# Rounding up the small tiles ahead of the matmul operands, so that every tile begins on a multiple of 64 bytes of a partition

## The chip, the cores and the metric

The kernel runs on one core of one Trainium2 chip. The metric is the device time of one execution in microseconds; lower is better. TensorE's clock has two levels, 1.2 and 2.4 GHz; the profile gives the granted share of full speed. Tiles lie in on-chip memory, 128 partitions side by side; a tile has the same start in every partition, and "where a tile begins" means its byte offset within a partition.

## The reference

Three modules in a row on 8 sequences of 576 tokens of width 512, all in fp32. The second module's two weights are multiplied by 8 in the inputs.

```python
def _attn_ref(q, k, v, g_norm):                 # 8 heads of 64
    kv = np.einsum('bhsd,bhse->bhde', k, v)
    out = np.einsum('bhsd,bhde->bhse', q, kv)
    rms = np.sqrt(np.mean(out * out, axis=-1, keepdims=True) + 1e-06)
    return (out / rms * g_norm).astype(np.float32)

def _moe_ref(x, w_ch1, w_ch2):                  # 512 -> 2048 -> 512
    X = np.fft.fft(np.fft.fft(x, axis=1), axis=2)
    u = x + np.real(X).astype(np.float32)
    un = (u - mean(u)) / np.sqrt(var(u) + 1e-06)
    return (u + np.maximum(un @ w_ch1, 0.0) @ w_ch2).astype(np.float32)

def _moe2_ref(x, U, V, w_ch1, w_ch2):           # rank 32 over the sequence
    h = x.transpose(0, 2, 1) @ U @ V
    u = x + h.transpose(0, 2, 1)
    return (u + np.maximum(u @ w_ch1, 0.0) @ w_ch2).astype(np.float32)
```

## The kernel before, in words

The 8 x 576 = 4608 tokens form 9 blocks of 512 (`BT`). The hidden width 2048 is cut into 16 slabs of 128 (`NF`). To keep fp32 accuracy with fast matmuls, each fp32 operand is split into a high part and a low remainder, both of type fp32r, and a product is three matmuls: low by high, high by low, high by high. Nearly all large matmuls therefore have 128x128 weights and stream 128x512 elements of 4 bytes.

**First transform (blocks 0 to 8).** For each of the 9 x 16 slabs `emit_l1` (L204) runs 12 matmuls: weights w1h and w1l, streamed xh and xl; ScalarE and VectorE make gh and gl from the result; `emit_l2` (L219) then runs 12: weights are slices of gl and gh, streamed w2h and w2l. Besides, ScalarE, VectorE and GpSimd split the weights of slabs to come, and beside each block of 16 slabs the attention and the Fourier transforms of the next sequence are placed (`batch_tasks`): t_kv, t_o, folds, two small DFT matmul stages against tables (t_s1, t_s2), and transposes of the normalized tokens (t_tr).

**Second transform.** Its first block, block 9 of the same loop, is plain: `emit_l1` streams xhb and xlb (tiles of pool `pb`) against w1h and w1l, and `emit_l2` now takes w2l, w2h as weights and streams gh, gl (L234 to L236). The other eight blocks go in four groups of two (`group`, L873), each with a fast 2x2 scheme of seven products instead of eight. A group's first phase (L953) has 56 units of 6 matmuls in the order `P1`: weights v, which are loaded from DRAM into five buffers of `pb`, streamed xv. There are seven variants p of xv (`XTAG`): 0, 1, 4 and 5 lie in pool `pa`, in the tiles xh, xl, res, un; 2, 3 and 6 in `pb`, in x0, x1, x2. p = 1 writes z, 3 and 6 write zz, the others y. ScalarE and VectorE (`post1`) empty the results into the 32 tiles of `wpool`. The phase ends with two units, (2, 7) and (6, 7), that follow each other. The second phase (L1033) has 56 units of 6 in the order `P2`: weights v, streamed high and low parts that `make` (L930) writes five units ahead (`LEAD`) into the buffers of w1h/w1l, w2h/w2l and gh/gl in turn, two buffers of each. In groups 1 to 3 the first phase also holds projecting matmuls of t_pt (L649: weights u1, streamed x2s), and units 2 to 9 of the second phase stand between transposes of t_u2 (L671, L674), all for the next group.

The order on every engine is that of the program's text (`tc.manual_schedule`): each engine goes through its list and waits where an operand isn't there. DMAs are issued by SyncE.

**Where tiles lie.** Pools are laid out one after the other in the order in which they are opened: com, wsp, gpool, pa, wpool, cvp and then at (attention), whose place pb takes later. In a pool tiles follow each other in the order of first use. Starts are rounded up to 32 bytes. com begins with ident (512 bytes), xe0 (96), nhalf (32), muT (144) and kvbd; because of the small ones, kvbd and all that follows in wsp, gpool and pa begins 32 bytes past a multiple of 64. pa ends with three small tiles (ln6, ln2, ln1: 96, 32, 16 bytes), after which wpool, cvp and pb begin on multiples of 64.

Of the kernel before, what the change touches and what calls it, by code (L numbers as in the profile page):

```python
# [10 lines left out]
F32 = mybir.dt.float32  # L11
F32R = mybir.dt.float32r
# [7 lines left out]
B, H, S, D = 8, 8, 576, 64  # L20
NH = S // 2 + 1
DM, DFF, RANK = 512, 2048, 32
NT = B * S
C = 128
RL = NH - 2 * C
NQ = 4 * C + 98
NS = 290
ND = 258
# [15 lines left out]
def kernel(ctx: ExitStack, tc: tile.TileContext, qT, kvm, gn, w1a, w2a, w1b, w2b,  # L44
# [4 lines left out]
    com = ctx.enter_context(tc.tile_pool(name="com", bufs=1))  # L49
# [7 lines left out]
    pa = ctx.enter_context(tc.tile_pool(name="pa", bufs=1))  # L57
    wpool = ctx.enter_context(tc.tile_pool(name="wpool", bufs=NF))
    cvp = ctx.enter_context(tc.tile_pool(name="cvp", bufs=1))

    early = [True]

    def side_bank(nm):
        if early:
            k = len(early) % 6
            early.append(True)
            if k < 4:
                return ps_acc.tile([128, 512], F32, tag=f"acc{k}", name=nm)
        return ps_s.tile([128, 512], F32, tag="side", name=nm)
# [6 lines left out]
    ub_d = [dram.tile([DM, BT], F32, tag=f"ub_d{j}", name=f"ub_d{j}") for j in range(1, NB)]  # L76

    ident = com.tile([128, 128], F32, name="ident")
    xe0 = com.tile([C, 3, B], F32, name="xe0")
    nhalf = com.tile([128, 8], F32, name="nhalf")  # L80
    muT = com.tile([128, NT // 128], F32, name="muT")


    def raw_load(src, n, where=None):
# [157 lines left out]
    at = att_ctx.enter_context(tc.tile_pool(name="at", bufs=1))  # L242
# [5 lines left out]
    def load_tables(step, t={}):  # L248

        for k, src in enumerate(tabs):  # L250
            if step == 0:
                t[k] = dram.tile(list(src.shape), F32, tag=f"tab_d{k}", name=f"tab_d{k}")
                nc.sync.dma_start(out=t[k], in_=src)
                continue
            s = at.tile(list(src.shape), F32R, name=f"tab{k}")
            nc.sync.dma_start(out=f32(s), in_=t[k])
            o = 0
            for nm, p, n in TABS[k]:
                tb[nm] = s[0:p, o:o + n]
                o += n  # L260
                if nm[1] in "sd":
                    tb[nm] = tb[nm].rearrange("p (k n) -> p k n", k=2)
# [24 lines left out]
    def t_o(b, k):  # L287
        s = st[b]
        g, c, m = OT[k]
        if k == 0:  # L290
            s["x"] = at.tile([C, 2, 3, DM], F32, tag="xpn", name=f"x{b}")
            s["sq"] = at.tile([C, 5, DM], F32, tag="slot_b", name=f"sq{b}")
            s["ss"] = at.tile([C, 5, H], F32, tag="ss", name=f"ss{b}", bufs=2)
        ps = side_bank(f"o{b}_{k}")
        for j in range(4):
            nc.tensor.matmul(out=ps[:m, 128 * j:128 * j + 128], lhsT=s["q"][:, j, C * k:C * k + m],  # L296
                             rhs=kvbd[:, j, :], start=True, stop=True)
        nc.scalar.activation(out=s["sq"][:m, k, :], in_=ps[:m, :], func=AF.Square)
        heads = lambda v: v.rearrange("p (h d) -> p h d", d=D)
        nc.vector.tensor_tensor(out=heads(s["x"][:m, g, c]), in0=heads(ps[:m, :]),  # L300
                                in1=gnb[:m].unsqueeze(1).to_broadcast([m, H, D]), op=ALU.mult)
        ss = s["ss"][:m, k]
        nc.vector.reduce_sum(out=ss, in_=s["sq"][:m, k].rearrange("p (h d) -> p h d", d=D), axis=AX.X)
        nc.vector.tensor_scalar(out=ss, in0=ss, scalar1=1.0 / D, scalar2=EPS, op0=ALU.mult, op1=ALU.add)
        nc.gpsimd.tensor_tensor(out=ss, in0=ss, in1=nhalf[:m, :], op=ALU.pow)
# [90 lines left out]
    def t_s2(b, c):  # L396
        s = st[b]
        m = min(C, NS - C * c)
        y = s["y"]
        pss = []  # L400
        for p in range(2):
            th, tl = (tb["cdh"], tb["cdl"]) if p == 0 else (tb["sdh"], tb["sdl"])
            ps = side_bank(f"s2_{b}_{c}_{p}")
            pss.append(ps)
            for ec in range(2):
                a, l = (y[:, p, k, ec, C * c:C * c + m] for k in range(2))
                nc.tensor.matmul(out=ps[:m, :ND], lhsT=l, rhs=th[:, ec, :], start=(ec == 0), stop=False)
                nc.tensor.matmul(out=ps[:m, :ND], lhsT=a, rhs=tl[:, ec, :], start=False, stop=False)
                nc.tensor.matmul(out=ps[:m, :ND], lhsT=a, rhs=th[:, ec, :], start=False, stop=(ec == 1))
        de = at.tile([C, 3, ND], F32, tag="de", name=f"de{b}_{c}", bufs=2)  # L410
        nc.scalar.activation(out=de[:m, 0], in_=pss[1][:m, :ND], func=AF.Copy)
        nc.vector.tensor_tensor(out=de[:m, 1], in0=pss[0][:m, :ND], in1=de[:m, 0], op=ALU.subtract)
        nc.vector.tensor_tensor(out=de[:m, 2], in0=pss[0][:m, :ND], in1=de[:m, 0], op=ALU.add)
        for g in range(2):
            x = s["x"][:m, g, c]
            eng = nc.vector if b == 0 and g == 0 else nc.gpsimd
            eng.tensor_tensor(out=x[:, 0:257], in0=x[:, 0:257], in1=de[:m, 1 + g, 0:257], op=ALU.add)
            eng.tensor_tensor(out=x[:, 257:512], in0=x[:, 257:512], in1=de[:m, 2 - g, 255:0:-1], op=ALU.add)
        if b:
            t_u_out(b, c)  # L420

    def t_u_out(b, c):
        s = st[b]
        n0, n1 = C * c, min(C * c + C, 289)
        nc.sync.dma_start(out=u_d[b][n0:n1, :], in_=s["x"][0:n1 - n0, 0, c])
        n0, n1 = C * c, min(C * c + C, 288)
        nc.sync.dma_start(out=u_d[b][288 + n0:288 + n1, :], in_=s["x"][n0 - C * c:n1 - C * c, 1, c])

    def load_q(b):
        q = at.tile([128, 4, NQ], F32, tag="slot_c", name=f"q{b}")  # L430
        nc.sync.dma_start(out=q, in_=qT[b])
        st.setdefault(b, {})["q"] = q

# [7 lines left out]
    def batch_tasks(b):  # L441

        t = [[] for _ in range(14)]
        d = SH if b == 1 else 0
        for c in range(3):
            ks = range(2 * c, min(2 * c + 2, 5))
            t[c + d] += [lambda k=k: t_o(b, k) for k in ks]
            t[c + d + 1] += [lambda k=k: t_norm(b, k) for k in ks]
            t[c + d + 3] += [lambda c=c, p=p: t_fold_s(b, c, p) for p in range(2)]
            t[c + d + 3] += [lambda c=c: t_fold_e(b, c, 0), lambda c=c: t_fold_h(b, c, 0)]  # L450
            t[c + d + 4] += [lambda c=c: t_fold_e(b, c, 1), lambda c=c: t_fold_h(b, c, 1)]
            t[c + d + 4] += [lambda p=p, c=c: t_fold_l(b, c, p) for p in range(2)]
            t[c + 9].append(lambda c=c: t_s2(b, c))
        for p in range(2):
            t[8 if d else 7 + p] += [lambda p=p, e=e: t_s1(b, p, e) for e in range(2)]
        if b + 1 < B:
            t[6 + d].append(lambda: load_kv(b + 1))
            t[11].insert(0, lambda: t_kv(b + 1, 0))
            t[12].insert(0, lambda: t_kv(b + 1, 1))
            t[12].append(lambda: load_q(b + 1))  # L460
        return t
# [18 lines left out]
    lns = {}  # L480
# [23 lines left out]

    def t_ln_stats(j, ts):
        if j not in lns:
            lns[j] = [pa.tile([128, 4, w], F32, tag=f"ln{w}", name=f"ln{j}_{w}") for w in (6, 2, 1)]
        st6, mv, rs = lns[j]
        for t in ts:
            nc.vector.bn_stats(out=st6[:, t, :], in_=un[j][t])  # L510
            nc.vector.bn_aggr(out=mv[:, t, :], in_=st6[:, t, :])
# [544 lines left out]
    with tc.manual_schedule():  # L1056
# [4 lines left out]
        nc.scalar.activation(out=e288, in_=f32(e288), func=AF.Copy)  # L1061
        load_kv(0)
        load_q(0)
        nc.sync.dma_start(out=gnb, in_=gn)
        load_tables(0)
        for s in range(4):
            w_load(s)
        load_tables(1)
        done = 0

# [8 lines left out]
        for k in range(5):  # L1079
            t_o(0, k)  # L1080
# [17 lines left out]
        conv_b(*conv_a(raws.pop(0), w_new(0), pws.pop(0)))  # L1098
        w_mags(1)
        t_s2(0, 2)  # L1100
        t_ln_first(2)
        t_s2(0, 0)
        t_ln_first(0)
        t_s2(0, 1)
# [5 lines left out]
        done = 2  # L1110
        load_kv(1)
        load_q(1)
        t_ln_stats(0, (0, 2))
        t_ln_stats(0, (1, 3))
        t_ln(0)
        for t in range(4):
# [67 lines left out]
        for n in range(NP):  # L1184
            i, j = n % NF, n // NF
# [136 lines left out]
```

## Time and profile before

| | |
|---|---|
| runs shown | 1823.01 us median of 3 (1821.85 to 1826.5) |
| profiled execution | 1822.28 us, of which the span of the trace is 1820.5 |
| mean granted clock | 0.982 |
| busy: PE, PEld, DVE, ACT, POOL | 95%, 79%, 65%, 46%, 26% of the span |
| DMA | 318 MB, 175 GB/s on average |
| stages, us from the span's start | first transform to 1052, block 9 to 1158, groups 1 to 4 from 1158, 1325, 1493 and 1659 |

PE is TensorE's matmul, PEld its weight load, which overlaps matmuls. A matmul's duration in the trace covers its way through the array, and the next one starts long before it ends; what counts in a stream is the distance between two starts. In the timeline and in the chain a row is one instruction or several of one kind merged (x6), with the first one's start and the time of all.

### The profile page before, as it was taken

To read this page: it belongs to the slowest core of one execution; us is meant where nothing else is said; L and a number is where in the kernel's file an instruction comes from. 1 tells how busy PE (TensorE), PEld (TensorE's weight loads), DVE (VectorE), ACT (ScalarE), POOL (GpSimd) and SP (SyncE) were. 2 spreads that over 40 slices of the span, in tenths; PEclk is the share of its full clock that TensorE was granted. 3 is DMA by queue.
4 is the path that set the end of the run, shared out by engine and by line. 5 is a ranking of instruction groups with operands and counts; after the bars stand their busy time and mean duration, and the time that the engine had idled before them with its cause. 6 is when DMAs were issued, how large, how long until landed. Compare 5 with 4: busy or idle time off the path is not lost.

```text
span 1820.5 us, 22972 instructions
## 1 busy us (share of the span) xinstructions
PE 1737.2 (95%) x8136; PEld 1432.6 (79%) x8136; DVE 1191.6 (65%) x1918; ACT 830.0 (46%) x1584; POOL 478.7 (26%) x384
## 2 busy tenths in 40 slices
PE   5678999999999999999999989999999999999999
PEld 5557778888787887878888868888887888888877
DVE  5787875857758586574476676637934873595285
ACT  4565343444534344343445466355535534453243
POOL 2556544454445544344222212100000000000000
PEclk7889999999999999999999999999999999999999
DMA  6735423143241513302258875566785776677675
GB/s 251 248 95 200 141 104 138 59 163 122 102 141 61 209 58 130 122 12 73 65 202 282 298 278 205 179 200 221 223 274 171 246 247 201 208 232 237 189 220 185
DMA packets 123731, 318.18 MB, mean 175 GB/s; under 512 B 18056, under 2 KB 20632, under 8 KB 120608
## 3 DMA queue, kind: packets, MB, share of 16 engines
q1 hardware_dynamic: 123616, 316.72, 52.2%
q8 instruction: 64, 1.05, 0.2%
q14 instruction: 51, 0.42, 0.1%
HBM read 241.13 MB, written 77.17 MB: 175 GB/s over the span
## 4 chain that ended last, share of the span: by engine, by line
PE 76%; DVE 12%; ACT 4%; DMA 3%; issue 2%; POOL 2%; SPq 1%; ACTq 0%; POOLq 0%; DVEq 0%
PE y L953 10%; PE yy L1033 10%; PE h L210 5%; PE h L212 5%; PE h L211 5%; PE acc L230 5%; PE acc L232 5%; PE z L1033 5%; PE acc L231 5%; PE zz L953 5%; PE z L953 2%; PE w L1033 2%; DVE f L335 2%; PE o L296 2%; DVE eh L364 2%
## 5 line engine op out<-in xcount | busy, mean ns | idle before, releaser
L188 POOL TENSOR_TENSOR w1l<-w,w1h 128x512 fp32r<-128x512 f32 x148 | 196.0, 1325 | 445.6 <-ACT w1h L187 422.2
L230 PE MATMUL acc<-w2h,gl 128*128 128x512 f32 x576 | 232.0, 403 | 28.8 <-DVE gl L216 28.7
L231 PE MATMUL acc<-w2l,gh 128*128 128x512 f32 x576 | 230.0, 399 | 8.4 <-POOL w2l L196 8.4
L210 PE MATMUL h<-xl,w1h 128*128 128x512 f32 x576 | 229.1, 398 | 1.4 <-DVE xl L533 1.4
L232 PE MATMUL acc<-w2h,gh 128*128 128x512 f32 x576 | 229.4, 398 | 0.0
L212 PE MATMUL h<-xh,w1l 128*128 128x512 f32 x576 | 225.5, 391 | 0.0
L211 PE MATMUL h<-xh,w1h 128*128 128x512 f32 x576 | 225.3, 391 | 0.0
L953 PE MATMUL y<-xv,v 128*128 128x512 f32 x768 | 192.2, 396 | 2.7 <-ACT g L890 2.7
L215 ACT ACTIVATE gh<-h 128x512 fp32r<-128x512 f32 x160 | 94.5, 591 | 179.6 <-PE h L212 177.3
L953 PEld LDWEIGHTS y<-xv,v 128*128 128x128 f32 x768 | 143.9, 188 | 38.9 <-ACT g L890 4.5
L216 DVE SCALAR_TENSOR_TENSOR gl<-h,gh 128x512 fp32r<-128x512 f32 x160 | 109.6, 686 | 98.8 <-ACT gh L215 98.5
L890 ACT ACTIVATE g<-y 128x512 f32<-128x512 f32 x128 | 76.6, 599 | 212.7 <-PE y L953 212.7
L196 DVE TENSOR_TENSOR w2l<-w,w2h 128x512 fp32r<-128x512 f32 x144 | 126.3, 877 | 48.9 <-ACT w2h L195 48.4
L230 PEld LDWEIGHTS acc<-w2h,gl 128*128 128x128 f32 x576 | 110.7, 192 | 60.1 <-DVE gl L216 37.1
L231 PEld LDWEIGHTS acc<-w2l,gh 128*128 128x128 f32 x576 | 110.6, 192 | 33.2 <-POOL w2l L196 11.0
L232 PEld LDWEIGHTS acc<-w2h,gh 128*128 128x128 f32 x576 | 111.0, 193 | 23.3
L212 PEld LDWEIGHTS h<-xh,w1l 128*128 128x128 f32 x576 | 108.5, 188 | 24.1
L210 PEld LDWEIGHTS h<-xl,w1h 128*128 128x128 f32 x576 | 108.8, 189 | 22.7 <-DVE xl L533 1.8
L211 PEld LDWEIGHTS h<-xh,w1h 128*128 128x128 f32 x576 | 108.7, 189 | 20.9
L195 ACT ACTIVATE w2h<-w 128x512 fp32r<-128x512 f32 x160 | 99.8, 624 | 38.9 <-PE acc L232 35.3
L187 ACT ACTIVATE w1h<-w 128x512 fp32r<-128x512 f32 x160 | 99.7, 623 | 14.7 <-DVE w L118 14.7
L884 DVE TENSOR_TENSOR g<-zz,g 128x512 f32<-128x512 f32 x64 | 44.2, 691 | 94.1 <-ACT g L890 80.7
(213 smaller groups left out, 3600.2 us busy)
## 6 DMA issues: line engine op xcount, KB each, us to landing
v<-wv_d SPq DMA_DIRECT2D x224, 512.0 KB, 4.0
wv_d<-vo SPq DMA_DIRECT2D x112, 256.0 KB, 2.8
kv<-in_kvm SPq DMA_DIRECT2D x14, 1280.0 KB, 9.4
q<-in_qT SPq DMA_DIRECT2D x8, 1220.0 KB, 9.3
x_d<-x2o SPq DMA_DIRECT2D x36, 256.0 KB, 2.1
x2f<-x_d SPq DMA_DIRECT2D x36, 256.0 KB, 5.2
outT<-o SPq DMA_DIRECT2D x36, 256.0 KB, 3.0
u_d<-x SPq DMA_DIRECT2D x32, 256.0 KB, 2.7
```

The source lines that it names most:

```text
L188: (nc.vector if n in on_dve else nc.gpsimd).tensor_tensor(out=al, in0=a, in1=f32(ah), op=ALU.subtract)
L195: nc.scalar.activation(out=ch, in_=c, func=AF.Copy)
L196: (nc.gpsimd if n in CLP else nc.vector).tensor_tensor(out=cl, in0=c, in1=f32(ch), op=ALU.subtract)
L210: nc.tensor.matmul(out=h, lhsT=ah[:, kc, :], rhs=xl[:, kc, :], start=(kc == 0), stop=False)
L211: nc.tensor.matmul(out=h, lhsT=ah[:, kc, :], rhs=xh[:, kc, :], start=False, stop=False)
L212: nc.tensor.matmul(out=h, lhsT=al[:, kc, :], rhs=xh[:, kc, :], start=False, stop=(kc == 3))
L216: nc.vector.scalar_tensor_tensor(out=gl, in0=h, scalar=0.0, in1=f32(gh), op0=ALU.max, op1=ALU.subtract)
L230: nc.tensor.matmul(out=a, lhsT=gl[:, tt], rhs=ch, start=s, stop=False)
L231: nc.tensor.matmul(out=a, lhsT=gh[:, tt], rhs=cl, start=False, stop=False)
L232: nc.tensor.matmul(out=a, lhsT=gh[:, tt], rhs=ch, start=False, stop=e)
L953: nc.tensor.matmul(out=dst, lhsT=w[:, c], rhs=r[:, k], start=p in (0, 1, 3) and k + n == 0, stop=k == 1 and n == 2, skip_group_check=True)
L1033: nc.tensor.matmul(out=dst[mp], lhsT=w[:, c], rhs=r, start=p in (0, 1, 6, 3) and i + n == 0, stop=i == 7 and n == 2, skip_group_check=True)
```

## The change: what it does

A helper, whole, allocates a tile with its row rounded up to 16 elements (64 bytes) and returns a view of the wanted part. It is used for xe0, nhalf, muT (pool com), ln6, ln2, ln1 (pa), and in at for the three tables, ss, de and q. No other tile changes its size. The views have the shape of the tiles before, so every instruction keeps its shape; and the engines' instructions stand in the same order, with the same waits. What changes is the start of tiles, here by its remainder modulo 64 bytes:

| tiles | before | after |
|---|---|---|
| kvbd; wsp: w1h, w1l, w2h, w2l; gpool: gh, gl | 32 | 0 |
| pa: xh, xl, un, res, x2o | 32 | 0 |
| wpool: w0, w1; cvp: raw, cv1 | 0 | 0 |
| at: gnb, e288, slot_a (kv, f), slot_c (q, y) | 0 | 0 |
| at: tables, x, slot_b (sq, eh), ez, one of the two de | 32 | 0 |
| pb: o, u1, x0, x1, x2, vs, v, x2f | 0 | 0 |

Among the tiles of wsp, gpool and pa the distances stay as they are. Rows within a tile keep their own offsets: 2048 or 512 bytes for the large operands, multiples of 8 bytes for some slices of the tables, of y and of q.

```diff
+    def whole(pool, shape, dt, name, tag=None, bufs=1):
+
+        n = int(np.prod(shape[1:]))
+        t = pool.tile([shape[0], -(-n // 16) * 16], dt, tag=tag or name, name=name, bufs=bufs)[:, 0:n]
+        if len(shape) == 2:
+            return t
+        names = "abcd"[:len(shape) - 1]
+        return t.rearrange(f"p ({' '.join(names)}) -> p {' '.join(names)}", **dict(zip(names, shape[1:])))
...
-    xe0 = com.tile([C, 3, B], F32, name="xe0")
-    nhalf = com.tile([128, 8], F32, name="nhalf")
-    muT = com.tile([128, NT // 128], F32, name="muT")
+    xe0 = whole(com, [C, 3, B], F32, "xe0")
+    nhalf = whole(com, [128, 8], F32, "nhalf")
+    muT = whole(com, [128, NT // 128], F32, "muT")
...
-            s = at.tile(list(src.shape), F32R, name=f"tab{k}")
+            s = whole(at, list(src.shape), F32R, f"tab{k}")
...
-            s["ss"] = at.tile([C, 5, H], F32, tag="ss", name=f"ss{b}", bufs=2)
+            s["ss"] = whole(at, [C, 5, H], F32, f"ss{b}", "ss", 2)
...
-        de = at.tile([C, 3, ND], F32, tag="de", name=f"de{b}_{c}", bufs=2)
+        de = whole(at, [C, 3, ND], F32, f"de{b}_{c}", "de", 2)
...
-        q = at.tile([128, 4, NQ], F32, tag="slot_c", name=f"q{b}")
+        q = whole(at, [128, 4, NQ], F32, f"q{b}", "slot_c")
...
-            lns[j] = [pa.tile([128, 4, w], F32, tag=f"ln{w}", name=f"ln{j}_{w}") for w in (6, 2, 1)]
+            lns[j] = [whole(pa, [128, 4, w], F32, f"ln{j}_{w}", f"ln{w}") for w in (6, 2, 1)]
```

## Rows read from the trace of the kernel before

**Rows 1.** The page: busy time of TensorE, granted clock in 40 slices.

```profile
PE 1737.2 (95%) x8136; PEld 1432.6 (79%) x8136; DVE 1191.6 (65%) x1918; ACT 830.0 (46%) x1584; POOL 478.7 (26%) x384
...
PEclk7889999999999999999999999999999999999999
```

**Rows 2.** The page: the chain that ended last, shares of the span by engine.

```profile
PE 76%; DVE 12%; ACT 4%; DMA 3%; issue 2%; POOL 2%; SPq 1%; ACTq 0%; POOLq 0%; DVEq 0%
```

**Rows 3.** TensorE's waits, whole run: total us, times, longest.

```profile
PE acc L230 <- DVE gl L216: 28.7, 20, 2.7
...
PE y L953 <- ACT g L890: 2.7, 4, 0.7
```

**Rows 4.** TensorE in order of time, first transform: start, us, instruction.

```profile
900.15 0.39 PE L232 MATMUL acc<-w2h,gh 128*128 128x512 f32 x1
...
903.55 0.39 PE L212 MATMUL h<-xh,w1l 128*128 128x512 f32 x1
```

**Rows 5.** The chain within group 4's second phase: start, us, instructions.

```profile
1749.48 11.20 PE z L1033 x48
```

**Rows 6.** Stretches: us, PE busy (instructions touched), clock, DMA share, GB/s.

```profile
880.00:948.00 68.00, 67.01 (x296) 1.00 0.50 163
1270.00:1321.00 51.00, 51.00 (x221) 1.00 0.72 224
```

**Rows 7.** TensorE in order of time, block 9, first and second layer.

```profile
1111.85 0.40 PE L211 MATMUL h<-xhb,w1h 128*128 128x512 f32 x1
...
1114.43 0.39 PE L234 MATMUL acc<-gh,w2l 128*128 128x512 f32 x1
...
1115.59 0.39 PE L236 MATMUL acc<-gh,w2h 128*128 128x512 f32 x1
...
1116.94 0.40 PE L236 MATMUL acc<-gh,w2h 128*128 128x512 f32 x1
```

**Rows 8.** The chain within group 1's first phase.

```profile
1167.59 1.41 PE z L953 x6
1168.99 1.39 PE zz L953 x6
```

**Rows 9.** TensorE in order of time, end of group 1's first phase.

```profile
1236.37 1.56 PE L953 MATMUL y<-xv,v 128*128 128x512 f32 x6
1238.62 1.64 PE L953 MATMUL y<-xv,v 128*128 128x512 f32 x6 [0.69 <-ACT g L890]
1240.10 1.52 PE L953 MATMUL zz<-xv,v 128*128 128x512 f32 x6
1241.46 0.40 PE L1033 MATMUL yy<-w1hg,v 128*128 128x512 f32 x1
```

**Rows 10.** TensorE in order of time, limits of first phases.

```profile
1157.65 0.63 PE L953 MATMUL y<-xv,v 128*128 128x512 f32 x2
...
1658.96 0.62 PE L953 MATMUL y<-xv,v 128*128 128x512 f32 x2
...
1738.10 0.40 PE L1033 MATMUL yy<-w1hg,v 128*128 128x512 f32 x1
```

**Rows 11.** Groups by line and form, VectorE: count, busy us, mean ns, idle before.

```profile
L887 DVE SCALAR_TENSOR_TENSOR g<-g,g 128x512 f32<-128x512 f32 x96 | 64.2, 683 | 0.0
...
L884 DVE TENSOR_TENSOR w2lg<-g,w2hg 128x512 fp32r<-128x512 f32 x52 | 35.9, 691 | 15.2 <-ACT w2hg L890 11.8
```

**Rows 12.** DMA issues: count, KB each, median us to landing.

```profile
o<-ub_d SPq DMA_DIRECT2D x32, 256.0 KB, 4.3
un<-u_d SPq DMA_DIRECT2D x28, 256.0 KB, 3.1
```

**Rows 13.** A stretch of group 4: busy PE, PEld, DVE, ACT, POOL, clock, DMA.

```profile
1745.00:1765.00 20.00, 20.00 (x88) 16.08 (x87) 19.38 (x32) 8.94 (x15) 0.00 (x0) 1.00 0.64 196
```

**Rows 14.** All engines in order of time, second phase of group 1.

```profile
1300.18 0.40 PE L1033 MATMUL yy<-ghg,v 128*128 128x512 f32 x1
...
1302.50 0.69 DVE L884 TENSOR_TENSOR glg<-g,ghg 128x512 fp32r<-128x512 f32 x1
```

## The prediction

> **What bounds the kernel now.** I read the shares first, then the chain, then what TensorE waits for, then the starts of its matmuls one by one. TensorE is busy 95% of the span and its granted clock stands at 90% or more of the upper level, 2.4 GHz, from the fourth of 40 slices on [rows 1]. The chain that ended last runs through PE for 76% [rows 2]. TensorE's waits are small: in the whole run the longest in total after the start are 28.7 us for gl (DVE) in the two-layer blocks, and in the 663 us of the four groups only 2.7 us, four times 0.7 us for ACT [rows 3]. So where TensorE doesn't wait, the time is the number of matmuls times the distance from the start of one to the start of the next, and this change alters no instruction, no wait and no order: it alters where tiles begin. The question is whether that distance depends on the place. The reader should therefore not look at the duration of a matmul (they overlap) but divide a stretch by its count.
>
> In the first transform's two layers both operands, weights and streamed tile, begin 32 bytes past a multiple of 64. From the matmul at 900.15 to the one at 903.55 there are 15 distances: 3.40 / 15 = 226.7 ns [rows 4]. In the second phase of a group the weights (v) begin on a multiple of 64 and the streamed tile 32 past one: pieces of 48 matmuls take 11.20 us, 233.3 ns each [rows 5]. Same shape, same clock of 1.00 [rows 5, 6]. The second transform's only plain block has both cases side by side. Its first layer streams xhb and xlb (multiples of 64) against w1h and w1l (32 past): the 11 distances from 1111.85 to 1114.43 are 2.58 us, 234.5 ns. Its second layer, straight after, streams gh and gl against w2h and w2l, both 32 past: the 6 distances from 1115.59 to 1116.94 are 1.35 us, 225 to 227 ns within the rounding [rows 7]. So it is not the stage; it goes with whether the two operands have the same place within 64 bytes.
>
> In the first phase of a group the weights are v (multiple of 64) and the streamed tiles are of both kinds, unit by unit: units that write z (32 past) take 1.41 us per six, those that write zz (multiples of 64) 1.39 [rows 8]: 234 and 231.7 ns. A zz unit has only six matmuls between units of the other kind. There is one place where both operands stay on multiples of 64 for longer: the last 12 matmuls of that phase. The first six need 1.48 us, with the settling after a wait; the next six, from 1240.10 to 1241.46, take 1.36 us, 226.7 ns [rows 9]. That is the number of the first transform. I read it so: matched operands run at 226.7 ns once they have settled, which takes a few matmuls; unmatched ones at 233.3 to 234.5; and it makes no difference whether both are on multiples of 64 or both 32 past.
>
> **The change part by part.** Every tile in question goes to a multiple of 64, so unmatched pairs become matched, and matched pairs stay so. Nothing is added to any engine or queue.
>
> Second phase of the groups (L1033): 4 x 336 = 1344 matmuls at 233.3 ns. In groups 1 to 3 eight units (48 matmuls) each have the transposes of t_u2 between them and never settle; I count 2 ns for these 144 and 233.3 - 226.7 = 6.6 ns for 1200: 7.9 + 0.3 = 8.2 us.
>
> First phase (L953): group 1's lasts from 1157.65 to 1241.46, 83.81 us, group 4's from 1658.96 to 1738.10, 79.14 us [rows 9, 10]. The difference is the 20 projecting matmuls of t_pt in group 1 (10 tasks of two). Group 2 has as many and group 3 half, so the four make about 2 x 83.8 + 81.5 + 79.1 = 328 us for 1344 + 50 = 1394 matmuls. All matched they are 1394 x 0.2267 = 316 us. The wait before the last 12 stays: there 2.25 us pass from 1236.37 to 1238.62 for six matmuls and 1.48 us for the next six, 1.0 us above 12 x 0.2267 [rows 9], so 4 us in four groups. 328 - 320 = 8 us. t_pt's own operands are on multiples of 64 already, so after the change they no longer break the run. I take 8.0.
>
> First layer of block 9 (L210 to L212 with xhb, xlb): 16 x 12 = 192 matmuls at 234.5 ns, less about 7 ns, some of it lost to settling after the transposes: 1.1 us; its second layer no longer has to settle after each change from one kind to the other: 0.2 us. Together 1.3.
>
> First transform: matched before and after, so nothing. Its small parts change partners, not kind: the tables and eh move together; the y slices against the second table meet the same set of offsets in another order; kvbd against q becomes matched, but its fp32 matmuls have 128 columns. I put these at 0, with 2 us either way.
>
> Other engines: an operation on 128x512 with two operands in SBUF takes 683 ns on DVE with all operands on multiples of 64 and 691 with two of them 32 past [rows 11]; a 256 KB load into un (32 past) lands in 3.1 us, one into o (multiple of 64) in 4.3 [rows 12]. If place had a price there, the rows would have it the other way about for the loads. I take 0 for both; the bound is 8 ns on the DVE operations, which stand off TensorE's path in the groups.
>
> What hides behind TensorE and could come out: in the second phase DVE is busy for 19.38 of 20 us at its fullest [rows 13]. With the phase 2.9% shorter that is 99.7%, still under. And it runs ahead: glg written from 1302.50 to 1303.19 replaces the tile that the unit at 1300.18 used, which comes up again six units of 1.4 us later, at 1308.6 [rows 14]; a lead of 5.4 us, against 2.2 us that a whole phase gets shorter. So I subtract nothing.
>
> Sum: 8.2 + 8.0 + 1.3 = 17.5 us. The profiled execution took 1822.28 us (span 1820.5), so 1804.8; the median of the runs shown, 1823.01, is 0.7 above it: **1805.5**.
>
> The Trainium skill speaks against the change. Its page "TensorE: Matmul & The Clock Gate", under "Step-by-step: what each phase is for", says that the two operands have read ports of their own and that "Loading the next tile's weights doesn't steal SBUF read bandwidth from the running matmul"; its page "SBUF — State Buffer", under "Door 1: The DMA port swizzle", gives lines of 16 bytes, of which 32 is a multiple. By either the place within 64 bytes would do nothing and the time would stay at 1823. The rows above disagree with that: 234.5 against 226.7 ns in neighbouring layers of one block [rows 7].
>
> **The rivals.**
> No effect (1823): the distance goes with what else runs, not with place. For it: the share of DMA is 0.50 in the stretch at 226.7 ns and 0.72 in the one at 233.3 [rows 6]. Against it: the two layers of block 9 alternate every few us in one environment and differ by 8 ns [rows 7], and the last 12 matmuls of a first phase run at 226.7 within a group [rows 9]. Chance 0.05.
>
> Given back (about 1814): DVE becomes the bound of the second phase, and its 8.2 us are lost. For it: 19.38 of 20 us [rows 13]. Against it: the lead of 5.4 us [rows 14]. The time would be 1805.5 + 8.2. Chance 0.04.
>
> Slower: multiples of 64 have a price of their own, and what one sees in a zz unit (231.7 ns [rows 8]) is their true distance in a stream, the last 12 of a phase being an exception. Then the first transform, 9 x 16 x 24 = 3456 matmuls, goes from 226.7 to 231.7, +17 us; the groups gain 1200 x 1.6 ns = 1.9 in the second phase, and in the first 1394 x 0.2317 + 4 = 327 against 328, 1 us; block 9's first layer gains 0.5. In all +14, some of it inside TensorE's waits in the first transform: about 1835. It decides from a distance of about 229.5 on: there 3456 x 2.8 ns = 9.7 us are lost and 1200 x 3.8 + 1394 x 2.9 + 192 x 5 ns = 9.6 won. Chance 0.04.
>
> **How the numbers follow.** Matched operands settle at 226.7: 0.87, 1805.5, with a range of its own from 1801 (transposes and short matmuls gain too, or t_pt's units settle at once) to 1810 (settling costs more than I took). No effect 0.05, given back 0.04, slower 0.04. Two medians of this kernel tell 0.3%, 5.5 us, from no change; faster by more is 0.87 + 0.04 = 0.91, within it 0.05, slower 0.04. The range for 8 in 10 is the likeliest's with the given-back case's near edge: 1801 to 1813.
>
> **What would show it.** In the profile after: pieces of 48 matmuls in a second phase at 10.88 us instead of 11.20; z and zz units alike at 1.36 us; first phases of about 81.7, 81.7, 79.4 and 77.2 us; the first layer of block 9 at 227 ns; the first transform's distances still 226.7; DVE's busy time unchanged, its share in the second phase near all, and TensorE's waits for it still none. The prediction is wrong if a second phase keeps 233 ns, if the first transform leaves 226.7, or if a wait for w1lg, w2lg or glg turns up on TensorE.

## The result, and the profile after

The changed kernel takes 1805.01 us (median of 5 runs, 1800.08 to 1805.89) against 1823.52 for the kernel before beside it (5 runs): ratio 0.9887, 95% interval 0.9868 to 0.9906. Predicted were 1805.5 and faster. That the two medians lie within 0.5 us is in part luck: the gain, forecast as 17.5 us, is 18.5 here and 20.9 in the second comparison (again, below). The profiled execution took 1800.08 us; its span is 22.2 us shorter than that of before (1820.5). All lines of code stand 9 lower now: L953 has become L962, L1033 L1042, L210 to L212 L219 to L221, L234 to L236 L243 to L245.

The page's head, busy times and clock, against [rows 1]:

```profile
span 1798.3 us, 22972 instructions
PE 1713.6 (95%) x8136; PEld 1429.1 (79%) x8136; DVE 1191.6 (66%) x1918; ACT 829.9 (46%) x1584; POOL 479.3 (27%) x384
PEclk8889999999999999999999999999999999999999
```

The counts of instructions are the same on every engine. TensorE's busy time fell by 23.6 us, which covers the whole difference; DVE's stayed at 1191.6. So the time came out of the matmuls, not out of waits. Where, the chain shows, in a second phase (start, us, instructions), against [rows 5]:

```profile
1729.20 10.88 PE z L1042 x48
```

10.88 us for 48 is 226.7 ns per matmul, 233.3 before. In a first phase, against [rows 8], units of z and zz are alike now, and 18 matmuls in a row take three times as long as six:

```profile
1161.71 1.36 PE z L962 x6
1163.07 1.36 PE zz L962 x6
...
1167.15 4.08 PE y L962 x18
```

The limits of first phases from TensorE's list in order of time, against [rows 9, 10] (start, us, instruction):

```profile
1152.03 0.39 PE L962 MATMUL y<-xv,v 128*128 128x512 f32 x1
...
1233.70 0.39 PE L1042 MATMUL yy<-w1hg,v 128*128 128x512 f32 x1
...
1641.02 0.39 PE L962 MATMUL y<-xv,v 128*128 128x512 f32 x1
...
1718.16 0.39 PE L1042 MATMUL yy<-w1hg,v 128*128 128x512 f32 x1
```

1233.70 - 1152.03 = 81.67 us in group 1 (83.81 before), 1718.16 - 1641.02 = 77.14 in group 4 (79.14 before). With the limits of the other groups read in the same way, the four first phases lost 8.4 us and the four second phases 8.2.

Block 9, in order of time: the start of its first layer and that of its second, 24 matmuls later; first before, then after.

```profile
1052.09 0.40 PE L210 MATMUL h<-xlb,w1h 128*128 128x512 f32 x1
...
1057.70 0.40 PE L234 MATMUL acc<-gh,w2l 128*128 128x512 f32 x1
```

```profile
1045.67 0.39 PE L219 MATMUL h<-xlb,w1h 128*128 128x512 f32 x1
...
1051.11 0.39 PE L243 MATMUL acc<-gh,w2l 128*128 128x512 f32 x1
```

The 24 distances took 5.61 us, 233.8 ns each, before and take 5.44 us, 226.7 ns, after. The starts are rounded to 0.01 us, which leaves some 0.4 ns either way in a figure from 24 distances.

The span's 22.2 us by stage, from the same starts (first slab 61.81 before and 60.51 after; block 9 1052.09 and 1045.67; groups 1157.65 and 1152.03): start 1.3, first transform 5.1, block 9 -0.8, groups and end 16.6.

TensorE's waits in the four groups (total us, times, longest) are the four for ACT that stood there before [rows 3], and no other:

```profile
PE y L962 <- ACT g L899: 2.7, 4, 0.7
```

### The profile page after: what moved, and what is told of

Read it like the earlier page. It is cut to its first block, busy times and chain, and to the rows that moved or that the text cites. A ratio compares the mean times of both kernels' runs of the same rounds, so it can differ in the third digit from the quotient of the medians.

```text
span 1798.3 us, 22972 instructions
## 1 busy us (share of the span) xinstructions
PE 1713.6 (95%) x8136; PEld 1429.1 (79%) x8136; DVE 1191.6 (66%) x1918; ACT 829.9 (46%) x1584; POOL 479.3 (27%) x384
## 4 chain that ended last, share of the span: by engine, by line
PE 75%; DVE 12%; DMA 4%; ACT 4%; issue 2%; POOL 2%; SPq 1%; ACTq 0%; DVEq 0%; POOLq 0%
PE y L962 10%; PE yy L1042 10%; PE h L219 5%; PE h L220 5%; PE h L221 5%; PE acc L239 5%; PE acc L241 5%; PE acc L240 5%; PE z L1042 5%; PE zz L962 5%; PE w L1042 2%; PE z L962 2%; DVE f L344 2%; DVE eh L373 2%; PE o L305 1%
## 5 line engine op out<-in xcount | busy, mean ns | idle before, releaser
L219 PE MATMUL h<-xl,w1h 128*128 128x512 f32 x576 | 228.3, 396 | 1.5 <-DVE xl L542 1.5
L221 PE MATMUL h<-xh,w1l 128*128 128x512 f32 x576 | 224.5, 390 | 0.0
L962 PE MATMUL y<-xv,v 128*128 128x512 f32 x768 | 187.4, 390 | 2.7 <-ACT g L899 2.7
L962 PEld LDWEIGHTS y<-xv,v 128*128 128x128 f32 x768 | 143.8, 188 | 34.1 <-ACT g L899 4.4
L221 PEld LDWEIGHTS h<-xh,w1l 128*128 128x128 f32 x576 | 108.5, 188 | 23.3
L219 PEld LDWEIGHTS h<-xl,w1h 128*128 128x128 f32 x576 | 108.8, 189 | 22.6 <-DVE xl L542 1.7
```

Of the source, the lines that this page charges most:

```text
L219: nc.tensor.matmul(out=h, lhsT=ah[:, kc, :], rhs=xl[:, kc, :], start=(kc == 0), stop=False)
L221: nc.tensor.matmul(out=h, lhsT=al[:, kc, :], rhs=xh[:, kc, :], start=False, stop=(kc == 3))
L962: nc.tensor.matmul(out=dst, lhsT=w[:, c], rhs=r[:, k], start=p in (0, 1, 3) and k + n == 0, stop=k == 1 and n == 2, skip_group_check=True)
```

## The experiments

Two theories stood at first. Mine: what counts is whether the two operands have the same place within 64 bytes. The rival: it is the multiples of 64 themselves. In the kernel after everything large is on a multiple of 64 and also matched, so it can't tell them apart. The mark of each run below is the time of 48 matmuls in group 4's second phase (start, us, instructions; 11.20 before, 10.88 after) and, where there are several runs, the ratio to the kernel before.

**com_only.** The change without the three small tiles at the end of pa, so that kvbd, wsp, gpool and pa come to 0 and what follows pa to 32.

```diff
-            lns[j] = [whole(pa, [128, 4, w], F32, f"ln{j}_{w}", f"ln{w}") for w in (6, 2, 1)]
+            lns[j] = [pa.tile([128, 4, w], F32, tag=f"ln{w}", name=f"ln{j}_{w}") for w in (6, 2, 1)]
```

> Half of the change: only xe0, nhalf, muT, the tables, ss, de and q are rounded up, not ln6, ln2, ln1 at the end of pool pa. So kvbd, wsp, gpool and pa begin on multiples of 64, and wpool, cvp, at and pb 32 past. Matching theory (the distance between matmul starts depends on whether weights and streamed tile have the same place within 64 bytes): the groups stream tiles at 0 against v at 32, the other way round than before, so a second phase keeps 11.20 us per 48 matmuls and a first phase about 83.8 us (79.1 in group 4); about 1823 us, no change from before. Absolute theory (what counts is that the streamed operand begins on a multiple of 64): the second phases fall to 10.88 us per 48, the first ones fall for variants 0, 1, 4 and 5; about 1808.

```profile
1746.13 11.20 PE z L1042 x48
```

1821.54 us, ratio 0.9989 [0.9977, 1.0001]. The large tiles of wsp, gpool and pa went to multiples of 64 and those behind pa left them, for nothing: the time is that of before within the interval.

**ln_only.** The other half: xe0, nhalf and muT as before, so that everything large stands 32 bytes past a multiple of 64.

```diff
-    xe0 = whole(com, [C, 3, B], F32, "xe0")
-    nhalf = whole(com, [128, 8], F32, "nhalf")
-    muT = whole(com, [128, NT // 128], F32, "muT")
+    xe0 = com.tile([C, 3, B], F32, name="xe0")
...
```

> The other half: only ln6, ln2, ln1 (and the tiles of pool at) are rounded up, not xe0, nhalf, muT. So every large tile, of all pools, begins 32 past a multiple of 64. Matching theory: all pairs match, 10.88 us per 48 matmuls in a second phase, first phases of 81.7 and 77.1 us, about 1805 us as with the whole change. Absolute theory (multiples of 64 are needed): nothing gained in the groups, 11.20 us per 48, about 1823.

```profile
1733.12 10.88 PE z L1042 x48
```

1803.0 us, ratio 0.9884 [0.9867, 0.9902]: the whole gain, with no large tile on a multiple of 64. The multiples themselves count for nothing; the place of the weights relative to the streamed tile does.

**v_64.** The kernel after, with the five v tiles 64 bytes into buffers that are 128 bytes longer. In a second phase v stands 64, 192, 64, 192 and 64 bytes (five buffers in turn) past the streamed tiles, modulo 256, and always at the same place within 64. The longer buffers also move x1 and x2, which lie behind v in pb, by 640 bytes, 128 modulo 256; the expectation has the streamed tiles staying where they are, which holds for those of a second phase alone.

```diff
-        t = vq[c] = pbx["pb"].tile([128, 2, 2, 256], F32R, tag="v", name=f"v{c}", bufs=5)
+        t = vq[c] = v_tile(f"v{c}")   # [128, 1024 + 32], view [:, 16:16 + 1024]
```

> The changed kernel with the weights v of the groups moved on: each buffer of v is 128 bytes longer and the weights begin 64 bytes into it, so that the five buffers begin at 64, 192, 320, 448 and 64 bytes of 512, while the streamed tiles stay on multiples of 256. Matching within 64 bytes: nothing changes, 10.88 us per 48 matmuls, about 1805. Matching within 128, 256 or 512 bytes (before, v and the streamed tiles stood 96 bytes apart of 512, after the change 0): the groups fall back to 11.20 us per 48 or a mixture, 1815 to 1825.

```profile
1742.79 11.10 PE z L1046 x48
```

1815.85 us, ratio 0.9961 [0.9949, 0.9973]. My criterion fails here: same place within 64 bytes, and yet 231.3 to 232.1 ns over 48 matmuls. Within such a piece the units differ; in order of time:

```profile
1745.38 0.39 PE L1046 MATMUL z<-w2hg,v 128*128 128x512 f32 x1
...
1749.58 0.39 PE L1046 MATMUL z<-w2hg,v 128*128 128x512 f32 x1
1750.97 0.39 PE L1046 MATMUL z<-ghg,v 128*128 128x512 f32 x1
...
1753.72 0.39 PE L1046 MATMUL yy<-w2hg,v 128*128 128x512 f32 x1
```

The first 18 distances are 4.20 us, 233.3 ns; the 12 from 1750.97 are 2.75 us, 229.2 ns. A buffer of v serves two units, and of every ten units six run at 232 to 233 ns and four at 229 to 230, as there are three buffers at 64 bytes and two at 192.

The moved x1 shows in block 9 that the price goes with the single pair. There xlb lies in x1, and xhb in x0, which is first used ahead of v and so stays:

```profile
1051.86 0.39 PE L221 MATMUL h<-xhb,w1l 128*128 128x512 f32 x1
1052.08 0.40 PE L219 MATMUL h<-xlb,w1h 128*128 128x512 f32 x1
1052.32 0.39 PE L220 MATMUL h<-xhb,w1h 128*128 128x512 f32 x1
```

Over the block, the median distance from a matmul that streams xlb to the next is 234 ns, from one that streams xhb 226 to 227.

**v_16.** The same with 16 bytes in place of 64 (16, 144, 16, 144 and 16).

```diff
-    [:, 16:16 + 1024]
+    [:, 4:4 + 1024]
```

> The changed kernel with the weights v of the groups 16 bytes past a multiple of 64 (in a buffer of 4224 bytes), the streamed tiles on multiples of 64. Matching theory, if any offset within 64 counts: 11.20 us per 48 matmuls, first phases of 84 to 85 us (now all seven variants unmatched), 1823 to 1826. Line theory (only the place within 16 bytes counts): unchanged, 1805. In between, if the distance grows with the offset: about 1814.

```profile
1743.88 11.20 PE z L1046 x48
```

1818.09 us, ratio 0.9967 [0.9954, 0.998]. All units of the second phase run at 233 to 234 ns: a shift by 16 bytes costs as much as one by 32. The time is some 5 us below the 1823 to 1826 expected; in the profile the groups are 1.7 us shorter than before and block 9 0.9, and the rest lies ahead of them.

**pb_32, pb_128, pb_192, pb_224.** The kernel after with a small tile ahead of cvp's others, which shifts cvp, at and pb by 32, 128, 192 or 224 bytes against wsp, gpool and pa; one run each, beside one of the kernel before at 1820.53.

```diff
+    cvp.tile([128, 8], F32, tag="pad", name="pad")      # 8, 32, 48 or 56 elements
```

> The changed kernel with 32 bytes more ahead of pool cvp: v, x0, x1, x2 and all of pb 32 bytes on, wsp, gpool and pa where they are. In a second phase every weight tile stands 32 past the streamed one (of 256 bytes). Both theories that are left, matching within 128 and within 256 bytes, expect about 11.2 us per 48 matmuls (16, 64, 144, 160 and 320 gave 233 ns); about 1820 us.

> The same with 128 bytes: weights 128 past the streamed tile. Matching within 128 bytes: 10.88 us per 48 matmuls in a second phase, groups of 642 us in all, about 1805 us. Matching within 256: more than 10.88, up to 11.20, and groups of 649 to 659 us; 1811 to 1820.

> The same with 192 bytes. In v_64 the matmuls whose weights stood 192 or 448 past the streamed tile took 228.9 ns on average, those at 64 or 320 took 233.3; but there the buffers alternate. If 228.9 is the place's own distance: 10.99 us per 48, groups of about 648 us, 1811 us. If it came from the alternation: 10.88 or 11.20.

> The same with 224 bytes (32 short of 256). If only the size of the shift counts, as 32: 11.2 us per 48, about 1820. If the direction counts (weights behind the streamed tile are cheaper, as 192 against 64): 10.9 to 11.0, about 1809.

In this order, from the four chains:

```profile
1746.04 11.20 PE z L1043 x48
```

```profile
1744.40 11.20 PE z L1043 x48
```

```profile
1742.06 10.99 PE z L1043 x48
```

```profile
1750.45 11.20 PE z L1043 x48
```

1818.86, 1817.2, 1813.59 and 1823.28 us. So 32, 128 and 224 bytes cost the same 6.6 ns, while 192 costs 2.3. Block 9 sees the same shifts the other way about, since there the streamed tiles (xhb, xlb) lie in pb and the weights in wsp: 32, 64, 128 and 224 bytes. Its first 24 distances, in pb_192 (64 bytes; in order of time):

```profile
1048.27 0.39 PE L219 MATMUL h<-xlb,w1h 128*128 128x512 f32 x1
...
1053.87 0.39 PE L243 MATMUL acc<-gh,w2l 128*128 128x512 f32 x1
```

5.60 us / 24 = 233.3 ns. Weights minus streamed tile, modulo 256 bytes, over all runs:

| bytes | 0 | 32 | 64 | 96 | 128 | 160 | 192 | 224 |
|---|---|---|---|---|---|---|---|---|
| ns, second phase | 226.7 | 233.3 | 233.3 (v_64) | | 233.3 | 233.3 (before) | 229.0 | 233.3 |
| ns, block 9 | 226.7 | 233.3 | 233.3 | 233.8 (before) | 232.9 | | | 233.8 |

It isn't a matter of how far apart the places are: 64 and 192 differ by their sign alone, 233.3 against 229.0, and v_64 has both in one stream. The figures at 32, 128, 192 and 224 are from one run each. And that 0 means modulo 256 and not 512 is seen in the kernel after itself: x0 stands 256 bytes from v there, modulo 512, and its units run at 226.7 like the others.

**w_64, w_32.** Does the reading of the weights set the distance? If it does, reading fewer should bring it down. In the kernel after, where all pairs match, six of the eight terms of a second phase, all but the first and the last, load only 64 (or 32) of 128 columns of weights. The rest of the output is left out, so each of these matmuls also writes fewer rows.

```diff
-                c = slice(128 * mp, 128 * mp + 128)
+                few = 64 if 0 < i < 7 else 128
+                c = slice(128 * mp, 128 * mp + few)
...
-                    nc.tensor.matmul(out=dst[mp], lhsT=w[:, c], rhs=r, start=...
+                    nc.tensor.matmul(out=dst[mp][0:few], lhsT=w[:, c], rhs=r, start=...
```

> The changed kernel, in which 36 of every 48 matmuls of a second phase load only 64 of their 128 weight columns (half of their output is left out; the streamed tile is whole, 512 columns). Theory that reading the next weights holds up the stream: the distance of these matmuls falls below 226.7 ns, to about 220 if what it loses goes with the columns read; pieces of 48 below 10.88 us, about 10.6. Theory that the distance is the stream's own and the weights only have to be ready: unchanged, 226.7 and 10.88.

> The same with 32 weight columns. Weights hold up the stream: about 217 ns, pieces of 48 at about 10.5 us. Stream's own distance: 226.7 and 10.88. The Trainium skill's page TensorE: Matmul & The Clock Gate, section Back-to-back issue gap, gives N / 2.4 + 2.5 ns, 215.8 for 512 columns, as the distance with nothing in the way; the first theory would come near it, the second not.

TensorE's list of w_64, from 12 matmuls with 64 columns to seven with 128:

```profile
1749.73 0.40 PE L1043 MATMUL yy<-w1hg,v 128*64 128x512 f32 x1
...
1752.49 0.39 PE L1043 MATMUL yy<-ghg,v 128*128 128x512 f32 x1
...
1754.08 0.39 PE L1043 MATMUL w<-w1lg,v 128*128 128x512 f32 x1
```

12 distances in 2.76 us, 230 ns, with the short loads; 7 in 1.59, 227.1 ns, with the full ones. Over 48 it is 11.00 us with 64 columns and 11.10 with 32, though the loads themselves got shorter (LDWEIGHTS, the weight loads, by form, of w_64 and then w_32; the second figure behind the bar is the mean: 188 ns for 128 columns, 134 for 64, 109 for 32):

```profile
L1043 PEld LDWEIGHTS yy<-ghg,v 128*64 128x64 f32 x128 | 17.2, 134 | 11.6
L1043 PEld LDWEIGHTS yy<-ghg,v 128*128 128x128 f32 x32 | 6.0, 188 | 1.5
```

```profile
L1043 PEld LDWEIGHTS yy<-ghg,v 128*32 128x32 f32 x128 | 13.9, 109 | 14.7
```

Single runs: 1803.59 and 1809.88 us, the kernel after beside them at 1801.88. Neither theory had the distance rise. With matched places, then, the amount of weights read is not what sets the 226.7 ns. Why fewer columns cost time isn't shown; columns read, length of the load and rows written changed together. Nor do these two runs say what collides where places don't match, since fewer columns were not tried there. One thing the profiles do show: in the second phases the load of 128 columns takes 188 ns before (unmatched) and after (matched) alike, so it is not the load that becomes longer. What inside TensorE or the memory makes the difference stays open.

**g_off.** Does the rule hold outside the groups? The kernel after with gh and gl (the weights of the first transform's second layer, and ghg and glg in the groups) 32 bytes into buffers 64 bytes longer.

```diff
-        gh = gpool.tile([128, BT], F32R, tag="gh", name=f"gh{n}")
+        gh = gpool.tile([128, BT + 16], F32R, tag="gh", name=f"gh{n}")[:, 8:8 + BT]
...
```

> The changed kernel with gh and gl alone 32 bytes on (each in a buffer 64 bytes longer, so 32, 96, 160 and 224 past a multiple of 256). This unmatches the second layer of the first transform (gh and gl are weights there), which the change left at 226.7 ns, and a third of the second phases' units. Matching theory: second layers at 233 to 234 ns, 1728 matmuls x 6.6 = 11 us, and 4 x 112 x 6.6 = 3 us in the second phases, less what lies in TensorE's waits: 1815 to 1820, slower than the changed kernel by 0.6 to 0.8%. If only the place of v in the groups mattered: about 1808.

1819.69 us, ratio 0.9986 [0.9976, 0.9995] to the kernel before, 17.8 us above the kernel after beside it (1801.88). In order of time, a second layer and the first layer that follows it:

```profile
900.13 0.40 PE L239 MATMUL acc<-w2h,gl 128*128 128x512 f32 x1
...
902.93 0.39 PE L219 MATMUL h<-xl,w1h 128*128 128x512 f32 x1
...
905.68 0.39 PE L239 MATMUL acc<-w2h,gl 128*128 128x512 f32 x1
```

2.80 us / 12 = 233.3 ns in the layer that was shifted, 2.75 / 12 = 229.2 in the one that was not and has to settle again. The first transform (from its first slab at 62.22 to block 9 at 1060.51) takes 998.3 us, 985.2 in the kernel after. Not all of these 13.1 us are the place's: the stretches 476.8 to 480.2, 698.7 to 702.1 and 811.3 to 814.7 ran at a granted clock of 0.50 to 0.51 here, and the kernel after has no counterpart to them. TensorE was busy throughout, so 10.2 us at half speed are 5.1 us lost, and about 8 are left for the place; 1728 x 6.6 ns would be 11.4, less what lies inside TensorE's waits. The groups are 5.0 us longer in the profile, which makes some 13 for the place in all, against 14 expected at most. In the groups ghg and glg are streamed from the same buffers, and 48 matmuls now take 11.04 to 11.12 us:

```profile
1747.55 11.12 PE z L1044 x48
```

**again.** The kernel after once more, unchanged, to see which of its stages vary.

> The changed kernel once more, for its ratio and a second profile. Pieces of 48 in a second phase at 10.88 us, the four groups 642 us together. If the runs at 1800 and at 1805 differ in how long the clock stays at its lower level at the start and in waits, the groups' time is the same in both, and the difference of this profile's span from 1798.3 is found in stretches before the groups with a lower granted clock.

```profile
1730.79 10.88 PE z L1042 x48
```

1801.88 us (4 runs, 1800.74 to 1802.75), ratio 0.9885 [0.9868, 0.9901]. The groups repeat: 642.1 us from their first matmul to their last in both profiles. What varies lies ahead of them: the first slab begins at 62.21 (60.51 in the first profile), and in block 9 another set of matmuls runs slower.

## Why the prediction was right

**The time and its terms.** Second phases 8.2 predicted, 8.2 measured. First phases 8.0 against 8.4. The limits predicted for them, 81.7 and 77.2 us in groups 1 and 4, came out as 81.67 and 77.14. These two terms were read from settled stretches of 12 to 48 matmuls at one clock, in which nothing but the place differed from the state to come, and they held.

**Block 9.** Its first layer went to 226.7 ns as predicted, but the stage became 0.8 us longer in the profiled execution instead of 1.3 shorter. The reason is in TensorE's list. Before, a wait of 3.34 us for x2s was followed by matmuls at the usual distance, nine distances in 2.11 us, 234 ns; after, a like wait was followed by slower ones. First before, then after:

```profile
1077.08 0.74 PE L649 MATMUL pt<-x2s,u 128*128 128x512 f32 x2 [3.34 <-DVE x2s L639]
1077.65 0.40 PE L210 MATMUL h<-xlb,w1h 128*128 128x512 f32 x1
...
1079.76 0.40 PE L210 MATMUL h<-xlb,w1h 128*128 128x512 f32 x1
```

```profile
1070.19 1.22 PE L658 MATMUL pt<-x2s,u 128*128 128x512 f32 x2 [3.30 <-DVE x2s L648]
1071.20 0.63 PE L219 MATMUL h<-xlb,w1h 128*128 128x512 f32 x1
...
1075.04 0.63 PE L219 MATMUL h<-xlb,w1h 128*128 128x512 f32 x1
```

Nine distances in 3.84 us are 427 ns, and the granted clock from 1071.2 to 1075.0 is 0.50, the lower of the two levels (stretch, PE busy, clock, DMA share, GB/s):

```profile
1071.20:1075.00 3.80, 3.80 (x10) 0.50 0.71 273
```

At 427 instead of 227 ns these nine alone cost 1.8 us, and the slab that they stand in became 2.0 us longer. The eleven slabs behind it, where both kernels run at the upper level, became 0.06 to 0.15 us shorter each, 1.2 together, and the first layers of the two at the start gained 0.17: the 1.3 predicted are there, and were outweighed by the clock. It was the execution before that was spared: behind that wait the first 12 matmuls run at 234 ns there, and at 321 to 427 ns on average in each of the other 13 profiles, that of com_only included, whose block 9 is unmatched as before. So the slow stretch doesn't come with the change.

**First transform.** Predicted at 0 with 2 us either way; in the profiles 990.3 and 985.2 us. Nearly all of the 5.1 us is the clock's. By the granted clock, TensorE stood at the lower level for 30.5 us of this stage before and for 20.5 after; most of these stretches lie at like places in both, and the three that only the kernel before has are (stretch, PE busy, clock, DMA share, GB/s):

```profile
61.80:65.00 3.20, 3.19 (x8) 0.50 0.94 395
201.50:204.90 3.40, 3.40 (x9) 0.50 0.02 5
696.50:699.90 3.40, 3.40 (x11) 0.50 0.39 78
```

10 us at half speed are 5.0 us lost. In settled stretches nothing changed; in order of time, after:

```profile
891.24 0.39 PE L219 MATMUL h<-xl,w1h 128*128 128x512 f32 x1
...
893.96 0.39 PE L239 MATMUL acc<-w2h,gl 128*128 128x512 f32 x1
```

2.72 us / 12 is 226.7 ns, as in [rows 4]. For the places of the small operands (kvbd, tables, y) next to nothing is left: with half of the time at the lower clock taken off, an estimate, the stage is 975.0 us before, 974.9 after, and 973.7 to 976.4 in the eleven other profiles that keep gh and gl in place. At the start of the run, where 1.3 us came from, none of the large matmuls lies. The profiled execution, 1800.08 us, stands 4.7 below the sum given for it, 1804.8: 1.3 and 5.1 there and 0.4 in the groups, less 2.1 in block 9. The runs of the kernel after spread from 1800 to 1806. That this spread is the clock's is argued from these profiles, not shown. The mean granted clock of the five goes the same way (0.985 at 1800.1 and 1800.4, 0.984 to 0.982 from 1805.0 to 1805.9), but one run of again has 0.982 at 1802.75.

**Where I was wrong: the criterion.** I took "the same place within 64 bytes" from two cases, 0 and 160 bytes (96 in block 9, where the two operands change sides), and it is the same place within 256. v_64 shows it: matched by my rule, 231.3 ns at best over 48. The number came out by luck, since the change happens to meet the right rule: ln6, ln2 and ln1 take 144 bytes before, rounded to 160 by the next pool's start, and 128 + 64 + 64 = 256 after. Rounding to 64 had no merit of its own; a fourth such tile would have made 320, 64 past, and the gain would have been near nothing, by the table above. It also means that the change's own description, multiples of 64, is not its cause: ln_only has the whole gain without one, com_only none with half of them.

**The rivals.** No effect: excluded by the ratio, and by com_only against ln_only, two kernels with the same traffic and a difference of 18.5 us. Given back by DVE: TensorE has no wait for it in the groups. Here I misread a row, though: 19.38 of 20 us was not the fullest stretch. Before, DVE was without idle time in the 20 us from 1741, and after for 24 us from 1719 (stretch of before; PE, PEld, DVE, ACT, POOL, clock, DMA share, GB/s):

```profile
1741.00:1761.00 20.00, 20.00 (x88) 16.08 (x87) 20.00 (x34) 9.14 (x15) 0.00 (x0) 1.00 0.69 215
```

A full DVE in a stretch was no bound: over the whole phase it is busy for 59.2 of 75.9 us, and in the groups TensorE waited for none of its results. That the lead of the forecast is what covered it fits, but was not tested apart. Slower by multiples of 64: the first transform kept 226.7 ns and com_only, where just its operands moved there, is not slower.

**What spoke against the change.** The Trainium skill gives TensorE's two operands read ports of their own ("TensorE: Matmul & The Clock Gate", "Step-by-step: what each phase is for") and the memory lines of 16 bytes ("SBUF — State Buffer", "Door 1: The DMA port swizzle"). By either, as the prediction read them, the place would do nothing. The trace disagrees, and it decides: 226.7 against 233.3 ns by place alone, and the same 233.3 at 16 and 144 bytes as at 32. Whether it is at the ports or the lines that the two operands meet, no run shows.

No version here beats the kernel after: 0 modulo 256 gave the shortest distance of all places tried.

## What to carry to other kernels

In a stream of 128x512 fp32r matmuls without waits, divide a stretch by its count: 226.7 ns or 233 ns at the same granted clock was here a matter of where weights and streamed tile begin, and 3% of the stream. Other shapes and types were not tried. Put both on the same place modulo 256 bytes, by padding ahead of a pool, and look again whenever a small tile is added ahead of either. A padding that does it for one pair can undo it for another (g_off), so each pair of operands has to be looked at by itself.

## What was not expected of the hardware

- The price of a place is nearly all or nothing: 6 to 7 ns at 32, 64, 96, 128, 160 and 224 bytes and at 16 and 144 in turn, 2.3 at 192, none at 0.
- Loading half or a quarter of the weight columns made the distance longer, 229.2 and 231.3 ns over 48, while the load itself fell from 188 to 134 and 109 ns.
- After a like wait of 3.3 us at the same place TensorE went on at the upper clock in one execution (0.23 us per matmul) and at the lower in another (0.43); in all, one profile of 14 was spared.
